# Splitting the first load over two queues and trimming warm-ups and tail of a gated attention and token-mixer kernel

## The chip, the cores and the metric

The kernel runs on one core of one Trainium2 chip. The metric is the device time of one execution in microseconds (us). The engines are named as in the profile: PE is TensorE's matmul side, PEld its weight loads, DVE is VectorE, ACT is ScalarE, POOL is GpSimd, and SP is SyncE, which here does nothing but issue transfers. An engine name with a q behind it (SPq, ACTq) is its sequencer, which issues transfers and waits.

## The reference

One input `x` of 2048 rows by 512 columns (bf16) goes through two blocks, and a gate mixes the results. Cut to what matters:

```python
x = A_x                                                # [1, 2048, 512]
g = sigmoid((x * gate_w).sum(-1, keepdims=True))
# block A: linear attention, 32 heads of 16
q, k, v = heads(x @ wqkv)
pq, pk = phi(q), phi(k)          # phi(t) = where(t > 0, t + 1, exp(t)) + 1e-6
kv, z = sum_s(pk * v), sum_s(pk)
a = ((pq @ kv) / (pq @ z + 1e-6)) @ wo
# block B: layer norm, then an MLP over the rows (tokens)
u = gelu(einsum("bsd,sf->bdf", layernorm(x), w1) + b1)   # f = 1792
b = transpose(einsum("bdf,fs->bds", u, w2) + b2)
out = g * a + (1 - g) * b
```

## The kernel before, in words

The 2048 rows are 16 tiles of 128 rows (`NT`), the 512 columns 4 chunks of 128 (`ND`). The order of all instructions is written out by hand, each engine runs its own in that order, and semaphores join them. There are four stages on PE:

1. For every row tile `t`: `k_part` multiplies the tile by Wk (four matmuls of 128x512, one for each chunk of Wk, into a bank `kacc`), `k_phi` turns it into `pk` on ACT and DVE, and `g_tile`, four tiles later, adds x^T pk into four banks `gacc`.
2. Three banks of the MLP's first layer (`uacc`) together with the q projection (`q_block`).
3. The rest of the first layer, and with it the small matmuls that fold Wv and Wo into `W2sb`.
4. For every row tile: four matmuls `aps` (attention) and 14 matmuls `yps` (the MLP's second layer), a DVE operation that mixes both into `ot` (line 501), and the store of `ot` (line 505). The last tile is done in column pieces, so that the last mix and store are short.

`k_part` needs the tile transposed (`xT`) as the stationary operand. Tiles 2 to 15 arrive transposed by transposing transfers that SP issues (`load_xT`, line 132). The first two tiles (`HEADS = 2`) are loaded plainly (`load_x`, line 126, into `xs`) and transposed on PE against the identity matrix (`transpose_part`, tile `pt`), then copied from PSUM to `xT` by DVE or ACT (`copy_part`, lines 203 and 205). The loop that does this:

```python
    for t in range(HEADS):
        for k0, k1 in ((0, 1), (1, 2), (2, ND)):
            transpose_part(t, k0, k1)
            copy_part(t, k0, k1, (t, k0) in ((0, 2), (1, 1)))
        k_part(0, range(2) if t == 0 else (2,))
    k_part(1, range(2))
    k_part(0, (3,))
```

So PE's order is: warm-up matmuls; transposes of tile 0; kacc of tile 0 with Wk's chunks 0 and 1; transposes of tile 1; kacc of tile 0 with chunk 2; kacc of tile 1 with chunks 0 and 1; kacc of tile 0 with chunk 3; kacc of tile 1 with chunks 2 and 3; tile 2. The warm-ups (`warm_up`, line 186) multiply a constant of ones into a bank that nobody reads. They need no transfer and run while the first ones are under way.

Transfers are issued from two queues, SP and ACT. SP issues x tile 0, x tile 1, Wk chunk 3, then the transposing loads; ACT issues Wk chunks 0 and 1 in one transfer, then chunk 2, then loads its table of functions (line 189). Below, x0 and x1 are the two plain x tiles, xT2 to xT5 the transposing loads that begin with tiles 2 to 5.

Of the kernel before, what the change touches and what calls it, by code (L numbers as in the profile page):

```python
# [15 lines left out]
def kernel(  # L16
# [13 lines left out]
    nc = tc.nc  # L30
    P = nc.NUM_PARTITIONS
# [6 lines left out]
    S, D = X.shape  # L38
    F = B_w1.shape[1]
    NT = S // P  # L40
# [12 lines left out]
    x_view = X.rearrange("(t p) d -> p t d", p=P)  # L53
# [12 lines left out]
    def keep(shape, dtype, name):  # L66
        return persist.tile(shape, dtype, name=name, tag=name)

    def bank(name, dtype=FP32):
        return ps.tile([P, SC], dtype, name=name, tag="bank")  # L70

    xs = keep([P, NT, D], BF16, "xs")
# [36 lines left out]
    def mm(o, lhsT, rhs, start, stop, **kw):  # L109
        nc.tensor.matmul(o, lhsT=lhsT, rhs=rhs, start=start, stop=stop, **kw)  # L110
# [14 lines left out]
    def load_x(q, t0, n):  # L125
        q.dma_start(out=xs[:, t0 : t0 + n, :], in_=x_view[:, t0 : t0 + n, :])

    def load_wk(q, k, n):
        q.dma_start(out=wk_sb[:, k : k + n, :], in_=wqkv_view[:, k : k + n, D : 2 * D])
# [3 lines left out]
            out=xT[:, :, t0 * P : (t0 + n) * P], in_=X[t0 * P : (t0 + n) * P, :], transpose=True  # L133
        )

    load_x(nc.sync, 0, 1)
    load_wk(nc.scalar, 0, 2)
    load_x(nc.sync, 1, 1)
    load_wk(nc.scalar, 2, 1)
    load_wk(nc.sync, 3, 1)  # L140
    for t in (2, 3, 4):
        load_xT(t, 1)
    nc.vector.memset(ones_f[:], 1.0)
# [3 lines left out]
        out=ident[:], in_=ident[:], compare_op=ALU.not_equal, fill=1.0, base=0,  # L147
# [5 lines left out]
        out=maskQ[:], in_=maskH[:].rearrange("p (a m) -> p m a", m=2), op=ALU.max, axis=AX.X  # L153
# [30 lines left out]
    def warm_up(n, cols=SC):  # L184
        for _ in range(n):
            mm(wps[:, :cols], warm[:, 0:P], warm[:, :cols], True, True)

    act_warm = keep([P, 1], FP32, "act_warm")
    nc.scalar.activation(out=act_warm[:], in_=ones_f[:], func=ACT.Exp)
    warm_up(6)  # L190

    pts = {}

    def transpose_part(t, k0, k1):
        pt = pts[t, k0, k1] = bank("pt")
        for k in range(k0, k1):
            mm(pt[:, k * P : (k + 1) * P], xs[:, t, k * P : (k + 1) * P], ident[:], True, True)

    def copy_part(t, k0, k1, on_act):
        src = pts.pop((t, k0, k1))[:, k0 * P : k1 * P].rearrange("p (k s) -> p k s", k=k1 - k0)  # L200
        dst = xT[:, k0:k1, t * P : (t + 1) * P]
        if on_act:
            nc.scalar.activation(out=dst, in_=src, func=ACT.Copy)
        else:
            nc.vector.tensor_copy(out=dst, in_=src)  # L205
# [13 lines left out]
    def k_part(t, ks):  # L219
        if t not in kaccs:  # L220
            kaccs[t] = bank("kacc")
        for k in ks:
            mm(
                kaccs[t][:], xT[:, k, t * P : (t + 1) * P], wk_sb[:, k, :],
                k == 0, k == ND - 1,
            )
# [55 lines left out]
    for t in range(HEADS):  # L282
        for k0, k1 in ((0, 1), (1, 2), (2, ND)):
            transpose_part(t, k0, k1)
            copy_part(t, k0, k1, (t, k0) in ((0, 2), (1, 1)))
        k_part(0, range(2) if t == 0 else (2,))
    k_part(1, range(2))
    k_part(0, (3,))
# [94 lines left out]
    def den_block(c, j):  # L383
        seg = pqT[:, j, c * SC : (c + 1) * SC]
        pz = work.tile([P, SC], FP32, name="pz", tag="pz", bufs=2)
        nc.scalar.activation(out=pz[:], in_=seg, func=ACT.Copy, scale=zcol[:, j : j + 1])  # L386
        nc.vector.transpose(out=zT[:], in_=pz[:])  # L387
        den = work.tile([P, SC // HEAD], FP32, name="den", tag="den", bufs=1)
        nc.vector.tensor_reduce(  # L389
            out=den[:], in_=zT[:].rearrange("p (a d) -> p a d", d=HEAD), op=ALU.add, axis=AX.X  # L390
        )
        rd = work.tile([P, SC // HEAD], BF16, name="rd", tag="rd", bufs=1)
        with nc.allow_low_precision(reason="the normalizer is used in bf16"):
            nc.vector.reciprocal(out=rd[:], in_=den[:])
        rex = work.tile([P, SC], BF16, name="rex", tag="rex", bufs=1)
        nc.vector.transpose(  # L396
            out=rex[:].rearrange("p (a d) -> p a d", d=HEAD),
            in_=rd[:].unsqueeze(2).to_broadcast([P, SC // HEAD, HEAD]),
        )
        nc.vector.tensor_tensor(out=seg, in0=seg, in1=rex[:], op=ALU.mult)  # L400
# [42 lines left out]
    for j in range(NB0, NF):  # L443
# [3 lines left out]
        for t in range(NT):  # L447
            if i == 2 and t < BRIDGE:
                for q in range(0, P, Q32):
                    c0 = jj * P + q  # L450
# [24 lines left out]
        out=gg[:], in0=gth[:], scalar1=0.5, scalar2=0.5, op0=ALU.mult, op1=ALU.add  # L475
    )
    nc.vector.tensor_scalar(
        out=c1[:], in0=gth[:], scalar1=-0.5, scalar2=0.5, op0=ALU.mult, op1=ALU.add
# [3 lines left out]
    for t in range(NT):  # L482
        c, tl = divmod(t, TPC)
        aps = bank("aps")
        for j in range(ND):
            mm(aps[:], pqT[:, j, t * P : (t + 1) * P], W2sb[:, j, :], j == 0, j == ND - 1)
        a_sc = work.tile([P, D], FP32, name="a_sc", tag="a_sc", bufs=2)
        nc.scalar.activation(  # L488
            out=a_sc[:], in_=aps[:], func=ACT.Identity,
            scale=gg[:, t : t + 1], bias=c2[:, t : t + 1],  # L490
        )
        for c0, W in ((0, 2 * P), (2 * P, P), (3 * P, P)) if t == NT - 1 else ((0, D),):
            cs = slice(c0, c0 + W)
            yps = bank("yps")
            for f in range(NF):
                mm(
                    yps[:, :W], w2c[c][:, f, tl * P : (tl + 1) * P], uT[:, f, cs],
                    f == 0, f == NF - 1,
                )
            ot = opool.tile([P, D], BF16, name="ot", tag="ot")  # L500
            nc.vector.scalar_tensor_tensor(  # L501
                out=ot[:, :W], in0=yps[:, :W], scalar=c1[:, t : t + 1], in1=a_sc[:, cs],
                op0=ALU.mult, op1=ALU.add,
            )
            (nc.scalar if t < 2 else nc.sync).dma_start(out=o_view[:, t, cs], in_=ot[:, :W])
        if t < NSC * ND - NDB:
            den_block(*divmod(t + NDB, ND))
# [30 lines left out]
```

## Time and profile before

| | us |
|---|---|
| median of 3 runs (162.43 to 162.89) | 162.76 |
| the profiled execution, its own time | 162.26 |
| its span, first to last instruction | 160.6 |
| PE matmuls busy | 155.9 (97% of the span) |
| DVE busy | 124.3 (77%) |
| ACT busy | 72.7 (45%) |
| PE warm-ups, six | 0.85 to 3.57 |
| start of the first transpose on PE | 3.36 |
| start of tile 2's kacc matmuls | 6.20 |
| start of the last DVE mix | 157.82 |

Times inside the execution count from the span's start. A matmul's bar in the trace is longer than the distance to the next one, because matmuls are pipelined: 128x512 matmuls have bars of 379 ns and start 216 ns apart. Of a transfer the profile gives the start of its issue and the time from there to its landing.

### The profile page before, as it was taken

What the parts mean: (1) busy time and instruction counts of PE and PEld (TensorE: products, weight loads), DVE (VectorE), ACT (ScalarE), POOL (GpSimd) and SP (SyncE); (2) the same over time, 40 slices, a digit from 0 to 9 for tenths busy, and PEclk for the clock granted to TensorE, in tenths of its full rate; (3) what the DMA queues carried; (4) which work ended last, traced back from release to release, by engine and by line L of the source; (5) the groups of instructions that cost most, each with busy time, mean ns of one, the idle gap of its engine ahead of it and who ended that gap; (6) DMA issues with size and microseconds to landing.
All of it is one profiled execution on the core that took longest, in us unless ns stands there. A gap on an engine that the chain in (4) does not pass through costs nothing.

```text
span 160.6 us, 2228 instructions
## 1 busy us (share of the span) xinstructions
PE 155.9 (97%) x822; PEld 72.5 (45%) x836; DVE 124.3 (77%) x274; ACT 72.7 (45%) x113; POOL 7.3 (5%) x17
## 2 busy tenths in 40 slices
PE   7999999999999999999999999999999999999993
PEld 2444444444444445444444444444444444444462
DVE  1599999769999998756999999676999999711122
ACT  3543486654978393059873320237333442111110
POOL 3000332002010000000000000000000000000000
PEclk9999999999999999999999999999999999999999
DMA  5699999999970007600930679401000001110001
GB/s 168 150 231 262 328 352 329 354 349 348 336 171 0 0 0 257 204 0 4 356 101 2 213 244 306 151 33 37 33 33 33 33 33 58 48 61 33 33 33 33
DMA packets 29929, 23.07 MB, mean 144 GB/s; under 512 B 8384, under 2 KB 29888, under 8 KB 29920
## 3 DMA queue, kind: packets, MB, share of 16 engines
q1 hardware_dynamic: 29104, 22.15, 45.2%
q10 hardware_dynamic: 704, 0.66, 1.2%
q0 software_dynamic: 112, 0.14, 0.4%
q8 instruction: 6, 0.10, 0.3%
q14 instruction: 3, 0.02, 0.0%
HBM read 19.01 MB, written 2.10 MB: 131 GB/s over the span
## 4 chain that ended last, share of the span: by engine, by line
PE 84%; DVE 13%; issue 1%; ACT 0%
PE yps L110 30%; PE uacc L110 24%; PE kacc L110 9%; PE gacc L110 9%; PE aps L110 9%; DVE pqT L213 6%; DVE zacc L274 3%; DVE stats L233 2%; DVE e L210 2%; PE wps L110 2%; PE qacc L110 1%; DVE mv L234 1%; ACT e L209 0%; PE kvps L110 0%; PE w2ps L110 0%
## 5 line engine op out<-in xcount | busy, mean ns | idle before, releaser
L110 PE MATMUL uacc<-hs,w1c 128*128 128x512 bf16 (+1 forms) x227 | 50.8, 379 | 0.4 <-issue 0.2
L110 PE MATMUL yps<-uT,w2c 128*128 128x512 bf16 (+2 forms) x247 | 50.8, 355 | 0.3
L110 PEld LDWEIGHTS <-w2c 128*128 128x128 bf16 x252 | 23.6, 98 | 25.2
L110 PEld LDWEIGHTS <-w1c 128*128 128x128 bf16 (+1 forms) x233 | 21.8, 98 | 26.0 <-issue 0.2
L488 ACT ACTIVATE a_sc<-aps,c,gg 128x512 f32<-128x512 f32 x16 | 12.4, 775 | 31.2 <-PE aps L110 15.5
L501 DVE SCALAR_TENSOR_TENSOR ot<-yps,c,a_sc 128x512 bf16<-128x512 f32 (+2 forms) x18 | 12.3, 688 | 15.3 <-PE yps L110 11.7
L322 ACT ACTIVATE uT<-uacc,bcol 128x512 bf16<-128x512 f32 x14 | 9.3, 686 | 17.5 <-PE uacc L110 17.4
L110 PE MATMUL qacc<-xT,wq_sb 128*128 128x512 bf16 x64 | 16.4, 379 | 0.1
L110 PE MATMUL aps<-W2sb,pqT 128*128 128x512 bf16 x63 | 16.4, 379 | 0.1
L110 PE MATMUL kacc<-wk_sb,xT 128*128 128x512 bf16 x63 | 15.9, 379 | 0.2 <-DVE xT L205 0.2
L387 DVE STREAM_TRANSPOSE zT<-pz 128x512 f32<-128x512 f32 x16 | 11.3, 705 | 6.0 <-ACT pz L386 6.0
L110 PE MATMUL gacc<-pk,xs 128*128 128x512 bf16 x63 | 15.7, 379 | 0.1
L249 ACT ACTIVATE hs<-xs,nmr,rstd 128x512 bf16<-128x512 bf16 x16 | 12.8, 805 | 2.3 <-DVE nmr L243 2.3
L209 ACT ACTIVATE e<-kacc 128x512 bf16<-128x512 f32 x16 | 9.4, 594 | 9.7 <-PE kacc L110 8.5
L386 ACT ACTIVATE pz<-pqT,zcol 128x512 f32<-128x512 bf16 x16 | 11.4, 715 | 4.8 <-DVE ot L501 4.7
L209 ACT ACTIVATE e<-qacc 128x512 bf16<-128x512 f32 x16 | 9.5, 594 | 7.7 <-PE qacc L110 7.7
L396 DVE STREAM_TRANSPOSE rex<-rd 128x512 bf16<-128x512 bf16 x16 | 11.4, 711 | 0.6
L213 DVE SCALAR_TENSOR_TENSOR pqT<-qacc,e 128x512 bf16<-128x512 f32 x16 | 11.1, 692 | 0.6
L213 DVE SCALAR_TENSOR_TENSOR pk<-kacc,e 128x512 bf16<-128x512 f32 x16 | 11.1, 692 | 0.6
L389 DVE TENSOR_REDUCE den<-zT 128x32 f32<-128x512 f32 x16 | 11.0, 686 | 0.6
L210 DVE TENSOR_SCALAR e<-e 128x512 bf16<-128x512 bf16 x32 | 9.0, 282 | 2.5 <-ACT e L209 2.5
L233 DVE BATCH_NORM_STATS2 stats<-xs 128x6 f32<-128x512 bf16 x16 | 10.9, 683 | 0.0
(58 smaller groups left out, 96.2 us busy)
## 6 DMA issues: line engine op xcount, KB each, us to landing
w2c<-in_B_w_dram SPq DMA_DIRECT2D x8, 896.0 KB, 5.7
w1c<-in_B_w_dram SPq DMA_DIRECT2D x3, 2048.0 KB, 14.0
out_dram<-ot SPq DMA_DIRECT2D x13, 128.0 KB, 1.7
xs<-in_A_x_dram SPq DMA_DIRECT2D x1, 1024.0 KB, 6.6
w1c<-in_B_w_dram SPq DMA_DIRECT2D x1, 1024.0 KB, 15.3
xs<-in_A_x_dram SPq DMA_DIRECT2D x1, 512.0 KB, 5.0
wq_sb<-in_A_wqkv_dram SPq DMA_DIRECT2D x1, 512.0 KB, 5.6
wv_sb<-in_A_wqkv_dram SPq DMA_DIRECT2D x1, 512.0 KB, 12.3
```

The source lines that it names most:

```text
L110: nc.tensor.matmul(o, lhsT=lhsT, rhs=rhs, start=start, stop=stop, **kw)
L209: nc.scalar.activation(out=e[:], in_=acc[:], func=ACT.Exp)
L210: nc.vector.tensor_scalar(out=e[:], in0=e[:], scalar1=1.0, scalar2=PHI_EPS, op0=ALU.min, op1=ALU.add)
L213: nc.vector.scalar_tensor_tensor(out=dst, in0=acc[:], scalar=0.0, in1=e[:], op0=ALU.max, op1=ALU.add)
L233: nc.vector.bn_stats(out=stats[:], in_=xs[:, t, :])
L249: nc.scalar.activation(out=hs[:, t, :], in_=xs[:, t, :], func=ACT.Identity, scale=rstd[:, t : t + 1], bias=nmr[:, t : t + 1],)
L386: nc.scalar.activation(out=pz[:], in_=seg, func=ACT.Copy, scale=zcol[:, j : j + 1])
L387: nc.vector.transpose(out=zT[:], in_=pz[:])
L389: nc.vector.tensor_reduce(out=den[:], in_=zT[:].rearrange("p (a d) -> p a d", d=HEAD), op=ALU.add, axis=AX.X)
L396: nc.vector.transpose(out=rex[:].rearrange("p (a d) -> p a d", d=HEAD), in_=rd[:].unsqueeze(2).to_broadcast([P, SC // HEAD, HEAD]),)
L488: nc.scalar.activation(out=a_sc[:], in_=aps[:], func=ACT.Identity, scale=gg[:, t : t + 1], bias=c2[:, t : t + 1],)
L501: nc.vector.scalar_tensor_tensor(out=ot[:, :W], in0=yps[:, :W], scalar=c1[:, t : t + 1], in1=a_sc[:, cs], op0=ALU.mult, op1=ALU.add,)
```

## The change

There are four edits. The first x tile is loaded as two halves of 64 rows, one from SP and one from ACT. Behind it each queue issues one of Wk's first two chunks, SP then x tile 1, ACT then Wk's chunks 2 and 3 in one transfer. The warm-ups ahead of the transposes are four of 512 columns and one of 384 instead of six of 512, and one more of 256 columns stands between the first tile's transposes and its kacc matmuls. The last output tile is done in pieces of 384 and 128 columns instead of 256, 128 and 128.

```diff
-    load_x(nc.sync, 0, 1)
-    load_wk(nc.scalar, 0, 2)
+    for q, p0 in ((nc.sync, 0), (nc.scalar, P // 2)):
+        q.dma_start(out=xs[p0 : p0 + P // 2, 0, :], in_=x_view[p0 : p0 + P // 2, 0, :])
+    load_wk(nc.sync, 0, 1)
+    load_wk(nc.scalar, 1, 1)
     load_x(nc.sync, 1, 1)
-    load_wk(nc.scalar, 2, 1)
-    load_wk(nc.sync, 3, 1)
+    load_wk(nc.scalar, 2, 2)
     for t in (2, 3, 4):
         load_xT(t, 1)
@@
-    warm_up(6)
+    warm_up(4)
+    warm_up(1, 384)
@@
             copy_part(t, k0, k1, (t, k0) in ((0, 2), (1, 1)))
+        if t == 0:
+            warm_up(1, 256)
         k_part(0, range(2) if t == 0 else (2,))
@@
-        for c0, W in ((0, 2 * P), (2 * P, P), (3 * P, P)) if t == NT - 1 else ((0, D),):
+        for c0, W in ((0, 3 * P), (3 * P, P)) if t == NT - 1 else ((0, D),):
```

## The prediction

> **What bounds the kernel now.** I read the page first: the share of each engine, then who TensorE (PE) waits for, then the first 7 us and the last 7 us of the timeline, then each early transfer's time to landing.
>
> ```profile
> PE 155.9 (97%) x822; PEld 72.5 (45%) x836; DVE 124.3 (77%) x274; ACT 72.7 (45%) x113; POOL 7.3 (5%) x17
> ```
>
> ```profile
> PE wps L110 <- PEq L522: 0.8, 1, 0.8
> PE kacc L110 <- DVE xT L205: 0.2, 1, 0.2
> PE uacc L110 <- issue: 0.2, 1, 0.2
> ```
>
> PE is busy 97% of the span, and its waits (last three rows) come to 1.2 us, of which 0.8 is the start of the program. So PE's queue is one unbroken chain: what moves the point from which it never waits again moves the end by the same amount. That point lies in the first microseconds of the timeline (columns: start, duration, engine and what it runs; in brackets the idle time before and what ended it):
>
> ```profile
> 0.85 2.72 PE L110 MATMUL wps<-const-bfloat16-1.0 128*128 128x512 bf16 x6 [0.85 <-PEq L522]
> 3.19 0.53 PEld L110 LDWEIGHTS <-xs 128*128 128x128 bf16 x4 [0.53 <-DMA xs<-in_A_x_dram]
> 3.36 0.53 PE L110 MATMUL pt<-ident,xs 128*128 128x128 bf16 x4
> 4.06 0.60 PE L110 MATMUL kacc<-wk_sb,xT 128*128 128x512 bf16 x2 [0.17 <-DVE xT L205]
> 4.50 0.39 PE L110 MATMUL pt<-ident,xs 128*128 128x128 bf16 x4
> 4.72 4.22 PE L110 MATMUL kacc<-wk_sb,xT 128*128 128x512 bf16 x18
> ```
>
> Six warm-ups hold PE to 3.36, although the x tile was there at 3.15 (the weight load of row 2 starts at 3.19). Then come four transposes, two kacc matmuls, the second tile's transposes at 4.50, kacc of Wk's chunk 2 at 4.72, and one more copy wait to 5.11; tile 2's first kacc matmul starts at 6.20 and nothing interrupts after it. Measure of the clock: warm-ups start 427 ns apart, kacc matmuls 216 ns; by the spacing of the four transposes the change comes at 3.65, 2.80 us after the first matmul.
>
> What feeds that stretch, as issue and time to landing (four windows of the DMA view):
>
> ```profile
> wk_sb<-in_A_wqkv_dram ACTq DMA_DIRECT2D x1, 256.0 KB, 3.1
> xs<-in_A_x_dram SPq DMA_DIRECT2D x1, 128.0 KB, 2.3
> ...
> xs<-in_A_x_dram SPq DMA_DIRECT2D x1, 128.0 KB, 3.0
> wk_sb<-in_A_wqkv_dram ACTq DMA_DIRECT2D x1, 128.0 KB, 3.3
> ...
> wk_sb<-in_A_wqkv_dram SPq DMA_DIRECT2D x1, 128.0 KB, 3.3
> ```
>
> With issues at 0.81, 0.81, 1.27, 1.30 and 1.73 the landings in the trace are: x0 3.15, Wk 0-1 3.87, x1 4.28, Wk 2 4.61, Wk 3 5.04. The same sums for the transposing loads, which SP issues 1.3 us apart from 2.20: xT2 5.75, xT3 6.31, xT4 7.54, xT5 9.27. Wk 2 is used 0.11 us after it lands, Wk 3 (at 5.55) 0.5 us after. The windows show what limits the landings:
>
> ```profile
> 1.80:2.20 0.40, 0.40 (x3) 0.13 (x2) 0.13 (x1) 0.38 (x1) 0.38 (x2) 1.00 0.49 125
> 2.20:2.60 0.40, 0.40 (x3) 0.12 (x2) 0.03 (x1) 0.40 (x1) 0.00 (x0) 1.00 0.78 246
> 2.60:3.00 0.40, 0.40 (x3) 0.06 (x1) 0.00 (x0) 0.40 (x1) 0.00 (x0) 1.00 1.03 356
> 3.40:3.80 0.40, 0.40 (x5) 0.32 (x3) 0.09 (x1) 0.00 (x0) 0.00 (x0) 1.00 1.09 382
> ...
> 89.70:90.10 0.40, 0.40 (x4) 0.20 (x2) 0.40 (x1) 0.28 (x1) 0.00 (x0) 1.00 0.62 184
> ```
>
> The last two columns are the DMA engines' share and GB/s. From 2.6 on the engines are full (356 to 382 GB/s) and only the bytes ahead of a transfer count; before that is a ramp at half rate. The last row, a W2 load that starts on idle engines from one queue, ramps in the same way.
>
> **The warm-ups.** 3072 columns become 2432: 640 columns at 427 ns per 512 is 0.53 us, so PE is free at 2.83 instead of 3.36. Behind them PE waits for both halves of x0. The other warm-up, 256 columns behind the first transposes, is 0.21 us at the slow rate; the first kacc waits 0.70 us after the first transpose (3.36 to 4.06) for the copy, the transposes take 0.43 of it, and it fits in the 0.27 left: nothing, as long as those 0.70 stay. The most that this part can give is 0.53.
>
> **x0 in two halves.** The bytes of x0 stay at 128 KB, and it now goes ahead of all of Wk. Call r the time by which the early transfers land sooner. Bounds: r = 0 if 16 engines work off the same rows in the same ramp; r = 0.6 if there were no ramp (x0's rows run from 1.84 to 2.79 in the trace; at 356 GB/s 128 KB need 0.37). I take 0.2, near the lower end, since the ramp shows in the single-queue load at 89.7 too, so it is not peculiar to x0, while Wk's 256 KB no longer compete in the first half microsecond. It could also be below nothing: one more transfer to complete, and PE waits for the later of two.
>
> The Trainium skill, "DMA: Bandwidth & Descriptors", section "Rules for kernel authors", speaks against this part: two transfers to disjoint partition halves serialize on the same 16 engines, one 128-partition transfer is better. By it r would be 0 and the sum below would end 0.2 later; no run so far shows two halves.
>
> **Wk and the order of queues.** SP's issues: x0a, Wk 0, x1, then xT2; ACT's: x0b, Wk 1, Wk 2-3. SP still makes three issues of 0.46 us before xT2, so the transposing loads keep their times to about 0.05. ACT makes three instead of two: its table load (1.28 us) starts at 2.3 instead of 1.82, so its first copy (0.38) can run from 3.85 and end at 4.25. That copy feeds the chunk-2 matmul; the landing of Wk 2 (below) covers it, and without that cover it would hold PE at 4.3. The 384 KB ahead of x1 are the same as before (x0 and Wk 0-1), so x1 lands at 4.28 - r. But Wk 2 and 3 are now one 256 KB transfer with one completion: chunk 2, which PE wants right behind the second transposes, comes with chunk 3, after the same 768 KB that stood before 5.04. It lands at 5.04 - r instead of 4.61.
>
> **Walking PE through it, r = 0.2.** x0 at 2.95, first transpose 3.0, first kacc 3.70, Wk 1 (3.87 - 0.2) is there, second kacc 3.93; x1 at 4.08, so the second transposes run at 4.14, with PE ready for Wk 2 at 4.37. Wk 2-3 land at 4.84, PE resumes at 4.88. The second tile's copies (0.61 us behind its transposes, 4.50 to 5.11) are done by 4.75. Six kacc matmuls of 216 ns remain to tile 2: 6.17, against 6.20. The 0.53 us of warm-ups turn into a wait for Wk: gain 0.03. With r = 0 it is 6.37, a loss of 0.18; with r = 0.4 5.97, a gain of 0.22.
>
> **The tail.** The last tile's 14 matmuls of 256 columns take 1.53 us and each 14 of 128 take 0.78 (starts 154.53, 156.06, 156.84). 384 columns lie between 109 and 216 ns a matmul: 162 ns, 2.27 us in place of 2.31. Gain 0.04. DVE's piece of 384 (0.62, between 0.48 and 0.75) ends at about 157.67, and the last piece starts at 157.79; SP's output issue (0.33) ends 0.1 before the last one. If either ran over, it would cost up to 0.1.
>
> **Sum.** -0.03 - 0.04 = -0.07 us. The profiled execution took 162.26 (span 160.6 and 1.66 around it), which becomes 162.19; the median is 162.76, 0.5 above, so the forecast is 162.7. That is no change: a difference of 0.3%, 0.49 us, is about what a measurement of this kernel can tell from none.
>
> **Rivals.** *Faster.* Two queues halve the ramp, r is 0.45 or more: PE then goes as early as the transposing loads allow. xT4 lands at 7.54, its matmul starts at 7.92; xT5 at 9.27 for 9.65. The gain stops at 0.34, up to 0.4 if SP's shorter first issue moves them; with the tail 162.3 to 162.4. For it: the ramp is real. Against: the row at 89.7.
>
> *Slower, x1 behind Wk 2-3.* ACT's third issue and SP's third start within 0.1 us of each other (about 1.70 on SP, 1.80 on ACT, by intervals of 0.46 and 0.49 to 0.52). If ACT's goes first, x1 lands where Wk 3 did, 5.04; transposes 5.08, copies to 5.69, where 5.11 was: 0.58 late, less the tail, 163.3. It decides when x1 lands later than 4.8. Against: landings so far follow the order of issue.
>
> *Slower, the clock.* Before the rate changes at 3.65, PE has run without a gap for 2.80 us. Now it idles between 2.83 and the landing of x0, 0.1 to 0.4 us. If a gap starts the count anew at 3.0, the fast rate comes at 5.8: the first four kacc matmuls and the second transposes run at half rate, to 5.85, four matmuls follow, and tile 2 starts at 6.71, 0.5 late: 163.2. It decides if such a gap counts at all; the 0.39 us between transposes and kacc, after the change, undid nothing. The Trainium skill, "TensorE: Matmul & The Clock Gate", Part 1, has a free-running window of about 3.4 us of activity that releases the clock; a full busy window cannot be needed, since the change came here after 2.80 us. Were a whole window lost, an estimate from that page's figure is twelve matmuls at the slow rate, 1.2 late, 163.9, which lies outside my range.
>
> **Chances.** Main case 0.55 (162.45 to 163.0), faster case 0.2, x1 late 0.13, clock 0.12. The faster case straddles the bound at 162.27; half of it and 0.1 from the scatter of the main case make 0.2 faster. Most of both slow cases, which end near the bound at 163.25 or beyond, and 0.05 from the main case's late end make 0.3 slower; 0.5 stay within 0.3%. The range runs from 162.2, the faster case, to 163.5, which takes in the late x1 and the shorter clock case.
>
> **What would show it.** Right: transposes at about 3.0, a wait of 0.3 to 0.7 us of kacc for Wk ahead of the third kacc matmul, tile 2 at 6.0 to 6.4, last output matmul about 0.04 nearer to the start of its tile. Wrong: Wk 2-3 landing before 4.5 with PE held by an xT load instead (faster), x1 landing after 4.8, or kacc matmuls 427 ns apart beyond 4 us (slower).

## The result, and the profile after

The changed kernel is slower: 165.15 us in the median of 6 runs (163.85 to 165.94), where before stands at 162.51 in the same comparison. The ratio is 1.0147, 95% interval 1.0113 to 1.0182, so about 2.4 us (the medians of these few runs lie 2.6 apart). The forecast of 162.7 and its range up to 163.5 missed. Ratios, here and below, are of fast runs: of one kernel, the halves by columns, two runs of ten stand over 1.5% above its fastest and are left out of its ratio. The profiled execution took 165.94 (span 164.2), 3.6 us more span than the one of before.

First the waits of PE (who waited for whom: total, times, longest), after:

```profile
PE wps L110 <- PEq L526: 0.8, 1, 0.8
PE pt L110 <- DMA xs<-in_A_x_dram: 0.8, 2, 0.5
PE kacc L110 <- DMA wk_sb<-in_A_wqkv_dram: 0.4, 1, 0.4
PE uacc L110 <- issue: 0.2, 1, 0.2
```

Where PE had one short wait for a copy, it now waits three times for transfers. (The view counts a wait from the modelled end of the matmul before it; by starts the gaps are larger.) The timeline shows the two queues and PE:

```profile
0.81 0.58 SPq L137 DMA_DIRECT2D xs<-in_A_x_dram  x1
0.81 0.57 ACTq L137 DMA_DIRECT2D xs<-in_A_x_dram  x1
...
1.41 1.08 ACTq L129 DMA_DIRECT2D wk_sb<-in_A_wqkv_dram  x2
1.45 0.83 SPq L129 DMA_DIRECT2D wk_sb<-in_A_wqkv_dram  x1
...
2.33 0.41 SPq L126 DMA_DIRECT2D xs<-in_A_x_dram  x1
...
3.49 0.59 PE L110 MATMUL pt<-ident,xs 128*128 128x128 bf16 x4 [0.46 <-DMA xs<-in_A_x_dram]
...
4.66 1.01 PE L110 MATMUL kacc<-wk_sb,xT 128*128 128x512 bf16 x2 [0.37 <-DMA wk_sb<-in_A_wqkv_dram]
...
6.03 0.61 PE L110 MATMUL pt<-ident,xs 128*128 128x128 bf16 x4 [0.36 <-DMA xs<-in_A_x_dram]
```

Three things differ from what the prediction took for granted. The two issues of half an x tile take 0.58 and 0.57 us, longer than a whole tile's 0.40, and the ordinary issue behind one takes up to 0.83, where 0.41 to 0.49 stood. So x1 is issued at 2.33, where I had 1.70, and ACT's Wk 2-3 (2.03) goes ahead of it. And the first transposes start at 3.49, later than before, in spite of shorter warm-ups.

The windows (last two columns: share of the DMA engines, GB/s) show that much less is then moved, where before 356 GB/s and more were reached from 2.6 on:

```profile
2.60:3.00 0.40, 0.40 (x2) 0.00 (x0) 0.00 (x0) 0.40 (x1) 0.00 (x0) 1.00 0.75 192
3.40:3.80 0.40, 0.31 (x4) 0.34 (x5) 0.01 (x1) 0.40 (x1) 0.00 (x0) 1.00 0.93 159
```

In these two stretches they move 192 and 159 GB/s, against 356 and 382 (between them 320, against 382). The engines still count as busy, 0.75 and 0.93, because single packets take long. In the DMA view of 3.4 to 3.8, 74 packets of ACT's queue take 51.5% of the time of 16 engines before, 45 ns each; after, six packets take 40.7%, 430 ns each on average. What held them the trace does not say.

The landings in the trace: x0's halves 3.05 and 3.35 (3.15 before), Wk 1 3.77, Wk 0 4.61, x1 5.98 (4.28), Wk 2-3 5.99 (Wk 2: 4.61, Wk 3: 5.04). The chain that ended last, from 0 to 12 us, names the transfer:

```profile
2.33 3.65 DMA xs<-in_A_x_dram
5.98 0.05 issue
6.03 0.61 PE pt L110 x4
6.63 5.53 PE kacc L110 x16
```

The last row holds the second half of the loss. In the groups of the page kacc matmuls have a mean bar of 426 ns (second row) where they had 379 (first row, before):

```profile
L110 PE MATMUL kacc<-wk_sb,xT 128*128 128x512 bf16 x63 | 15.9, 379 | 0.2 <-DVE xT L205 0.2
L110 PE MATMUL kacc<-wk_sb,xT 128*128 128x512 bf16 x63 | 18.3, 426 | 0.4 <-DMA wk_sb<-in_A_wqkv_dram 0.4
```

By their starts they stand 427 ns apart until 10.70 and 216 after: the fast rate comes 7 us later than the 3.65 of before. (The columns PEclk do not show this; they read full speed throughout.) The sum for the profiled execution: the second transposes start 1.53 us later (6.03 for 4.50); ten kacc matmuls and four transposes behind them run at the slow rate, 10 x 0.211 + 0.2 = 2.3, and the copy wait of before, 0.17, is hidden. That is 3.65, which is what the first gacc matmul shows (12.43 for 8.79) and what is handed on to the end of the span (3.64).

### The profile page after: what moved, and what is told of

Read it like the earlier page. It is cut to its first block, busy times and chain, and to the rows that moved or that the text cites. A ratio compares the mean times of both kernels' runs of the same rounds, so it can differ in the third digit from the quotient of the medians.

```text
span 164.2 us, 2199 instructions
## 1 busy us (share of the span) xinstructions
PE 158.5 (97%) x808; PEld 72.3 (44%) x822; DVE 124.2 (76%) x273; ACT 72.8 (44%) x113; POOL 7.3 (4%) x17
## 4 chain that ended last, share of the span: by engine, by line
PE 81%; DVE 13%; DMA 2%; issue 1%; SPq 1%; ACT 0%
PE yps L110 29%; PE uacc L110 23%; PE kacc L110 9%; PE gacc L110 8%; PE aps L110 8%; DVE pqT L215 5%; DVE zacc L276 3%; DMA xs<-in_A_x_dram 2%; DVE stats L235 2%; DVE e L212 2%; PE qacc L110 1%; DVE mv L236 1%; SPq L129 1%; PE pt L110 0%; ACT e L211 0%
## 5 line engine op out<-in xcount | busy, mean ns | idle before, releaser
L110 PEld LDWEIGHTS <-w2c 128*128 128x128 bf16 x238 | 22.8, 98 | 25.9
L110 PE MATMUL kacc<-wk_sb,xT 128*128 128x512 bf16 x63 | 18.3, 426 | 0.4 <-DMA wk_sb<-in_A_wqkv_dram 0.4
L110 PEld LDWEIGHTS <-xs 128*128 128x128 bf16 x72 | 7.0, 101 | 10.0 <-DMA xs<-in_A_x_dram 2.5
```

## The experiments

Every time is compared with runs of before on the same chip. Two theories stood at the start. *C*: the loss is mainly the late fast rate, brought on by PE's idle time. *T*: the late transfers alone make it.

**Loads alone.** The new loads, with the warm-ups and the tail of before.

```diff
-    load_x(nc.sync, 0, 1)
-    load_wk(nc.scalar, 0, 2)
+    for q, p0 in ((nc.sync, 0), (nc.scalar, P // 2)):
+        q.dma_start(out=xs[p0 : p0 + P // 2, 0, :], in_=x_view[p0 : p0 + P // 2, 0, :])
+    load_wk(nc.sync, 0, 1)
+    load_wk(nc.scalar, 1, 1)
     load_x(nc.sync, 1, 1)
-    load_wk(nc.scalar, 2, 1)
-    load_wk(nc.sync, 3, 1)
+    load_wk(nc.scalar, 2, 2)
```

> The new order of loads alone, with the six warm-ups and the tail of before. Theory C (most of the loss is the clock: PE's gap between the shorter warm-ups and x0 postpones the fast rate): warm-ups run to 3.36, the rate changes near 3.65 as before, and only the later landings cost; from the trace of after x1 lands at about 6.0 instead of 4.3, so about +1.5 us, 164.0. Theory T (the late transfers alone make the loss, the slow rate only follows from them): the same as the whole change, 165.2. If the issues from two queues did not disturb each other after all: 162.5.

Measured: 164.17 (163.78 to 165.71), ratio 1.0112 (1.0057 to 1.0166). The loads by themselves carry most of the loss, as far as four runs tell. In this profile the transposes start at 3.36 as before, but Wk holds PE at 5.17 and 6.71, and the fast rate is there from 4.9 on.

**Warm-ups alone.**

```diff
-    warm_up(6)
+    warm_up(4)
+    warm_up(1, 384)
...
+        if t == 0:
+            warm_up(1, 256)
```

> The shorter warm-ups alone (four of 512, one of 384, one of 256 behind the first transposes), with the loads and tail of before. Theory C: PE idles from 2.83 to 3.19, the rate changes one window of some 3.5 us later or more, kacc at 427 ns until about 7, +1.2 to +2 us: 163.7 to 164.5. Theory T: x0 lands at 3.15, PE starts up to 0.17 earlier, 162.4 to 162.6.

Measured: 162.77, ratio 1.0003 (0.9984 to 1.0021). C's number is wrong here: PE idles for about 0.3 us before x0 and nothing is lost. Nothing is won either; in the profile the first kacc starts at 4.02, when Wk 0-1 is there (3.98), and what follows runs at the slow rate to 5.39. A rival of mine, that this gap alone would cost 0.5 us or more, falls.

**The whole change with PE kept busy.**

```diff
-    warm_up(4)
-    warm_up(1, 384)
+    warm_up(7)
...
+        if t == 1:
+            warm_up(3)
...
-            warm_up(1, 256)
+            warm_up(1, 512)
```

> The whole change, but with PE kept busy: seven warm-ups of 512 ahead of the first transposes, one of 512 behind them and three of 512 ahead of the second tile's transposes. Theory C: the rate changes near 3.65, the transfers still cost about 1.5: 164.0, and kacc matmuls stand 216 ns apart from the first one. Theory T: no better than the whole change, 165.2 or later.

Measured: 164.41 (164.03 to 165.02), ratio 1.0122 (1.0086 to 1.0157). No run reaches the 165.5 to 165.9 of half of the runs of the whole change, which is C's side; four runs are few for that. The fast rate came at 5.24, not at 3.65. About 2 us stay. Most of that is the transfers: x1 lands at 5.85, and the added warm-ups themselves hold the second transposes from there to 6.10.

**The split alone.** x0's halves, then Wk and x1 on the queues of before.

```diff
-    load_x(nc.sync, 0, 1)
+    for q, p0 in ((nc.sync, 0), (nc.scalar, P // 2)):
+        q.dma_start(out=xs[p0 : p0 + P // 2, 0, :], in_=x_view[p0 : p0 + P // 2, 0, :])
```

> The split of x0 alone: two halves from SP and ACT, then Wk 0-1, x1, Wk 2, Wk 3 on the queues of before, warm-ups and tail of before. If it is the two simultaneous issues that cost (0.58 us each in the trace of after where 0.40 and 0.46 stood), x1 is issued 0.2 to 0.5 later and lands at 4.6 to 5.0, and tile 2 starts 0.3 to 0.6 later: 162.9 to 163.2. If it is the order of Wk instead, no change: 162.5.

Measured: 165.49 (164.47 to 166.09), ratio 1.0169 (1.0119 to 1.0219), far more than expected. The two lines of the split cost as much as the whole change. The issues again take 0.58 and 0.57, ACT's next one 0.85, and Wk 0-1 lands at 5.95 instead of 3.87, so that PE stands from 3.78 to 5.99. The fast rate is there when it goes on (second row below):

```profile
3.36 0.63 PE L110 MATMUL pt<-ident,xs 128*128 128x128 bf16 x4
5.99 0.59 PE L110 MATMUL kacc<-wk_sb,xT 128*128 128x512 bf16 x2 [2.00 <-DMA wk_sb<-in_A_wqkv_dram]
```

In this kernel x1, issued at 1.44 behind SP's half, lands at 3.81, earlier than before (4.28): it is not always the same transfer that comes late. What is slow about it: 64 rows (*R*), or two queues that begin with a half (*Q*)?

**Halves by columns.** Against the split alone:

```diff
-    for q, p0 in ((nc.sync, 0), (nc.scalar, P // 2)):
-        q.dma_start(out=xs[p0 : p0 + P // 2, 0, :], in_=x_view[p0 : p0 + P // 2, 0, :])
+    for q, c0 in ((nc.sync, 0), (nc.scalar, D // 2)):
+        q.dma_start(out=xs[:, 0, c0 : c0 + D // 2], in_=x_view[:, 0, c0 : c0 + D // 2])
```

> x0 in two halves from SP and ACT as in split_only, but cut by columns: each half has all 128 rows, 256 columns of each. Theory R (a transfer to 64 partitions is slow to issue): the first issues take 0.40 to 0.46 us again, x1 is issued near 1.27 and lands near 4.4; ACT's Wk comes one issue later, so 162.5 to 163.2. Theory Q (two queues that begin with a half each, and one more transfer, are slow whatever the cut): issues of 0.58 and 0.85 as in split_only, 164.5 or more.

Measured: 163.4, ratio 1.0073 (1.0028 to 1.0118), in two groups: six runs from 162.97 to 163.47, four from 165.18 to 165.69 (the ratio is without the highest two). The lower group lies at the upper end of what R was given, the upper one above Q's bound. The queues, by columns:

```profile
0.80 0.41 ACTq L137 DMA_DIRECT2D xs<-in_A_x_dram  x1
0.81 0.40 SPq L137 DMA_DIRECT2D xs<-in_A_x_dram  x1
1.24 0.99 ACTq L129 DMA_DIRECT2D wk_sb<-in_A_wqkv_dram  x2
1.27 0.41 SPq L126 DMA_DIRECT2D xs<-in_A_x_dram  x1
```

**Both 64-row halves on one queue.** Against the split alone:

```diff
-    for q, p0 in ((nc.sync, 0), (nc.scalar, P // 2)):
-        q.dma_start(out=xs[p0 : p0 + P // 2, 0, :], in_=x_view[p0 : p0 + P // 2, 0, :])
+    for p0 in (0, P // 2):
+        nc.sync.dma_start(out=xs[p0 : p0 + P // 2, 0, :], in_=x_view[p0 : p0 + P // 2, 0, :])
```

> x0 as two halves of 64 rows, both from SP; ACT begins with Wk 0-1 as before, SP goes on with x1 and Wk 3. Theory R: SP's two first issues take 0.58 each, x1 is issued at 2.0 or later and lands above 5: 163.5 to 164.5. Theory Q: SP's issues take 0.40 to 0.46, x1 is issued at 1.74 and lands near 4.4: 162.6 to 163.0.

Measured: 165.68 (165.18 to 166.01), ratio 1.0193 (1.016 to 1.0227). The queues:

```profile
0.80 1.00 ACTq L129 DMA_DIRECT2D wk_sb<-in_A_wqkv_dram  x2
0.81 1.21 SPq L137 DMA_DIRECT2D xs<-in_A_x_dram  x2
2.06 0.58 SPq L126 DMA_DIRECT2D xs<-in_A_x_dram  x1
```

With the same bytes, halves by columns are issued in 0.40 and 0.41 on two queues at once; halves by 64 rows take 0.58 and 0.57 on a queue of their own, and so does the x1 behind them (0.58), while ACT's issues beside them keep their usual 0.5. For the issues this is R. The time itself is 1.2 us above what R was given; with x0 late, the fast rate comes only at 9.7 in this profile. x0 lands at 4.30 and 4.97 here, and at 2.9 and 3.06 by columns. On two queues the 64-row halves landed 2.2 and 2.5 us after the start of their issues (whole change; 2.3 for the whole tile before), here 3.5, behind Wk 0-1, which was issued in 0.48 beside them and landed at 4.00, ahead of x0.

**Wk 2 and 3 merged, alone.**

```diff
-    load_wk(nc.scalar, 2, 1)
-    load_wk(nc.sync, 3, 1)
+    load_wk(nc.scalar, 2, 2)
```

> Loads of before with one difference: Wk's chunks 2 and 3 in one transfer from ACT. By the step of the prediction, they land together near 5.0, chunk 2 is wanted at 4.72, tile 2 starts 0.1 to 0.3 later; the transposing loads are issued 0.46 earlier, which brings nothing: 162.6 to 163.0. If the merge were a main part of the loss: above 163.5.

Measured: 162.9, ratio 1.0016 (0.9997 to 1.0035): as the prediction had it, with Wk 2-3 landing at 4.99 and the third kacc at 5.03, where 4.72 stood.

**The whole change without the split.**

```diff
-    for q, p0 in ((nc.sync, 0), (nc.scalar, P // 2)):
-        q.dma_start(out=xs[p0 : p0 + P // 2, 0, :], in_=x_view[p0 : p0 + P // 2, 0, :])
-    load_wk(nc.sync, 0, 1)
-    load_wk(nc.scalar, 1, 1)
-    load_x(nc.sync, 1, 1)
-    load_wk(nc.scalar, 2, 2)
+    load_x(nc.sync, 0, 1)
+    load_wk(nc.scalar, 0, 1)
+    load_wk(nc.sync, 1, 1)
+    load_wk(nc.scalar, 2, 2)
+    load_x(nc.sync, 1, 1)
```

> The whole change without the split: x0 in one transfer from SP, Wk 0 from ACT, Wk 1 and x1 from SP, Wk 2-3 from ACT, the shorter warm-ups and the tail of 384 and 128. Theory S (the split is the cause of the loss): issues of 0.4 to 0.5, 162.5 to 163.1. If Wk's new order or the shorter warm-ups carry the loss: 163.8 or more, as the whole change.

Measured: 163.68 (163.25 to 165.05), ratio 1.0071 (1.003 to 1.0112), between the two expectations. ACT, with one issue less ahead, now issues Wk 2-3 at 1.25 and SP x1 at 1.73; x1 lands at 5.30 behind it and the second transposes start at 5.35, 0.85 late. This is the prediction's rival of x1 behind Wk 2-3, in a kernel of its own.

**The gap filled.** Halves by columns as above, and PE busy while it waits for Wk:

```diff
             copy_part(t, k0, k1, (t, k0) in ((0, 2), (1, 1)))
+        if t == 0:
+            warm_up(2)
```

> column_halves with two more warm-ups of 512 columns behind the first tile's transposes, where PE waited 0.75 us for Wk. The runs of column_halves fall into two groups, 163.0 to 163.5 (six) and 165.2 to 165.7 (four). Theory C (the upper group is a fast rate that comes a window or two late, because PE was idle in the window): with the gap filled no run is above 164.5, median 163.0 to 163.5. If the upper group comes from the transfers: it stays, in about four runs of ten.

Measured: 163.55 (163.05 to 163.99), ratio 1.0035 (1.0018 to 1.0052). None of 12 runs is in the upper group, where four of ten were; chance alone would do that about 3 times in 100. The transfers land within 0.2 us of those of the column cut, so the upper group goes with PE's idle time of 0.76 us ahead of the first kacc. That it is the clock's is likely but was not seen, since no run of the upper group was profiled. The lowest run, 163.05, is still 0.8 above the lowest of before (162.29), with the gap filled: that is mainly the transfers' part.

**Two warm-ups.** Before with four warm-ups less.

```diff
-    warm_up(6)
+    warm_up(2)
```

> Before with two warm-ups instead of six, transfers untouched: PE idles from 1.70 to x0's landing at about 3.1. Theory C: the fast rate comes late in many runs, 164 to 165.5, kacc matmuls 427 ns apart to 6 us or beyond. If gaps don't count and only time since the first matmul does: 162.5 to 163.0.

Measured: 163.95 (163.19 to 164.74), ratio 1.0067 (1.0045 to 1.009). PE idles from about 1.7 to 3.21; kacc matmuls stand 427 ns apart to 7.4. Idle time with untouched transfers costs 1.1 us, just under the lower end of C and without its 165s.

**The whole change with halves by columns.** The one difference from the whole change is the cut.

```diff
-        q.dma_start(out=xs[p0 : p0 + P // 2, 0, :], in_=x_view[p0 : p0 + P // 2, 0, :])
+        q.dma_start(out=xs[:, 0, c0 : c0 + D // 2], in_=x_view[:, 0, c0 : c0 + D // 2])
```

> The whole change with one difference: the halves of x0 are cut by columns (128 rows, 256 columns each) instead of by 64 rows. Theory R (64-row transfers are slow to issue, and what follows them): first issues of 0.40, x1 issued at 1.7 instead of 2.3, landing near 5.0 instead of 6.0; lower group at 162.8 to 163.4, with some runs 2 us above it from the clock. Without R: as the whole change, lower group 163.9.

Measured: 163.34, ratio 1.0037 (1.0012 to 1.0063); nine of ten runs from 162.97 to 163.67, one at 165.31. The cut by 64 rows thus makes 1.1% of the 1.47%, about 1.8 us. (That is a difference of two ratios from two comparisons, good to some 0.4%.) x1 is issued at 1.72 and lands at 4.89. In the profile of this kernel the first kacc still waits for Wk, to 4.32, and the second transposes start at 5.12: transfers that land later than before make the remaining 0.6 us, together with the clock (fast rate from 5.6).

**The tail alone.**

```diff
-        for c0, W in ((0, 2 * P), (2 * P, P), (3 * P, P)) if t == NT - 1 else ((0, D),):
+        for c0, W in ((0, 3 * P), (3 * P, P)) if t == NT - 1 else ((0, D),):
```

> The tail of 384 and 128 columns alone. By the step of the prediction 0.04 us sooner, which a comparison of medians can't tell from nothing; the time from the last tile's first yps matmul to the end of the span should be 0.03 to 0.05 shorter: 6.03 instead of 6.07.

Measured: 163.07, ratio 1.0001 (0.9982 to 1.0019). From the last tile's last aps matmul to its last yps matmul 3.216 us pass, 3.252 before: 0.04 sooner, as forecast, and too little for the medians to tell. By the measure that was named, from the first yps matmul to the end of the span, nothing is gained: 6.07, against 6.03 before. The last store is issued 0.04 sooner but lands at the same distance from that matmul (5.11 before, 5.10 here). The profile of this run has a use beyond its question (PE's timeline):

```profile
3.36 0.63 PE L110 MATMUL pt<-ident,xs 128*128 128x128 bf16 x4
4.05 1.03 PE L110 MATMUL kacc<-wk_sb,xT 128*128 128x512 bf16 x2
4.88 0.63 PE L110 MATMUL pt<-ident,xs 128*128 128x128 bf16 x4
5.31 1.91 PE L110 MATMUL kacc<-wk_sb,xT 128*128 128x512 bf16 x5
```

The start is that of before, to the instruction and to 0.01 us up to 4.05. But here the matmuls stay 427 ns apart until 6.6, and the execution took 163.53 where the profiled one of before, with the fast rate from 3.65, took 162.26. The moment of the fast rate is not a property of the kernel.

No kernel here beats the one of before.

## Why the prediction was wrong, point by point

**What held.** That PE's first 6 us set the end: every shift of the first gacc matmul is found again at the end of the span (3.65 in, 3.64 out; in all fourteen profiles to within 0.3). The tail: 0.04 forecast, 0.04 measured on PE, of which nothing was left at the end, and DVE's piece of 384 took 0.62 as estimated. The merge of Wk 2 and 3: 5.04 - r forecast, 4.99 measured. That shorter warm-ups only turn into a wait for Wk: no change when done alone.

**The step that failed first** is "SP still makes three issues of 0.46 us before xT2". An issue was priced by the rows of 128-row transfers, and the 64-row one was even given a gain ("SP's shorter first issue"). It takes 0.58, and the issue behind it 0.56 to 0.86. x1 was issued at 2.33 instead of 1.70, and xT2 at 2.79 instead of 2.20.

**The step that failed with it** is "only the bytes ahead of a transfer count". From it x1 was put at 4.28 - r, that is 4.08, and it landed at 5.98: issued 0.63 late, and then 3.65 us on the way where 2.38 were allowed. Wk 2-3 going ahead explains 0.76 of that by the prediction's own rows (5.04 for 4.28). The rest it does not explain: the same 768 KB were through at 5.99, not at 5.04 - r.

**The term r** stands for that step. It had bounds of 0 and 0.6 and I took 0.2, with one clause that it could also be below nothing and no price for that. It was below: the last of the early transfers landed at 5.99 instead of 5.04, r = -0.95. Halves by columns still give -0.4 (Wk 2 at 5.47 as the last of the same bytes). The missing bound would have been the cost of a stretch at a low rate, and the rows for it stood in the prediction's own window view: the ramp at 125 and 246 GB/s. In the whole change low rates last until 4.2 us (187 GB/s from 3.8 to 4.2). The slow issues have a large part in that; what of it comes from the larger number of smaller transfers, as in the column cut with its normal issues, was not separated.

The Trainium skill, "DMA: Bandwidth & Descriptors", "Rules for kernel authors", which spoke against the split, was right in its advice. Its reason, that the halves serialize on the same engines, would give r = 0; the measured loss is larger, and begins with the issue of 64-row transfers.

**The rival of x1 behind Wk 2-3** came true in the whole change, but by a cause not thought of: not because ACT's third issue was early (2.03, 0.23 later than I had it), but because SP's was 0.63 late. Its price of 0.58 was too small; x1 landed at 5.98, not 5.04. The order is not all of it either: with the loads alone SP's x1 went first (2.06, ACT's third at 2.30) and still landed at 5.46.

**The rival of the clock** came true as well, and not as told. The fast rate is not counted from PE's first matmul: with the same start it came at 3.65 in one execution and at 6.6 in another. A gap of 0.3 us before x0 does nothing (ratio 1.0003). But idle time while the rate is still slow makes it possible to miss the change again, until 9.7 (both halves on one queue) or 10.7 (the whole change). In the main sum the clock stood at nothing. The rival's price, 0.5, was counted from a restart at 3.0; the profile shows 2.1 on the kacc matmuls alone, and the two groups of the column cut stand 2.3 apart. What the Trainium skill's "TensorE: Matmul & The Clock Gate", Part 1, says of a window that runs freely and so differs from run to run agrees with 3.65 and 6.6 for one start, though the spread measured here is larger than the 0.5 us to either side that the part gives. I had used the page's window for a price beyond my range and let the trace's 2.80 us decide, which is one draw from a spread. That price does not come out either: twelve matmuls at 0.211 are 2.5 us, not 1.2, and nothing is said of what would hide the rest.

**The chances.** The two slow rivals were treated as alternatives of 0.13 and 0.12. They share a cause: a late x1 leaves PE idle, and idle PE keeps the slow rate. Added up they are 1.5 + 2.1, which no case held.

**What stays open.** Why a 64-row transfer is slow to issue, and slows the one behind it, was not found out. That the upper runs of the whole change (165.46 to 165.94) are the clock's rests on the profile of one of them (165.94, fast rate from 10.70); the filled version of the whole change had four runs only. How much idle time in which stretch delays the fast rate is settled only in part (last section): 0.3 us before x0 cost nothing, 0.76 behind it brought four runs of ten to 165, 1.5 before it cost 1.1 on average.

## What to carry to other kernels

Price an issue by a row of the same shape, and where there is none, leave room for it to be slower. A transfer cut by rows is not half a transfer; if a first tile must be cut for two queues, cut its columns and keep all 128 partitions. Here even that was slower than no cut, by 0.73% alone and 0.35% with the gap filled. In a kernel whose start is a race between loads and warm-ups, let PE do idle work until the loads have arrived: a wait there can cost more in clock than its own length.

## What the runs showed of the hardware

Among the first loads, issues of 64-row transfers of 64 KB from SP or ACT took 0.57 to 0.58 us, of 128-row transfers of 64 or 128 KB 0.40 to 0.43 from SP; the 128-row issue behind a 64-row one on its queue took 0.56 to 0.86. The first loads of the kernel before moved 125 GB/s from 1.8 to 2.2, 246 from 2.2 to 2.6 and 356 from then on; a later load on idle DMA engines moved 184 in the 0.4 us from 89.7 and 302 in the next.

The fast rate of PE came at 3.65 and at 6.6 with the same instructions and loads, worth 1.1 us at the first gacc matmul (8.79 and 9.86). The kernel of before ranged from 162.29 to 163.41 in 35 runs, a spread of the same size; it would fit that the profiled execution, with its early change, lay 0.5 below the median shown.

The traces say more of when that change comes. Twelve of the fourteen hold a record of the granted clock, which begins at the change (3.65 before, 10.70 in the whole change); the fast stretch in it lasts 157.013 us in ten kernels and 153.600 in two, that is 46 and 45 times 3.4133. Count back from the change in steps of 3.413 us, and take a matmul of 512 columns at the slow rate as 0.427 us of work:

| | change at | busy in the step before it | in earlier steps |
|---|---|---|---|
| before | 3.65 | 82% | |
| tail alone | 6.64 | 92% | 70% |
| merge alone | 3.47 | 77% | |
| whole change by columns | 5.63 | 74% | 40% |
| both halves on one queue | 9.69 | 100% | 41%, 59% |
| whole change | 10.70 | 100% | 67%, 69% |

In all twelve the step that ended in the change was 74 to 100% busy, and no earlier step more than 70%. This fits a clock that is judged at fixed steps of 3.413 us, which fall differently on every execution: in the tail alone a step ended at 3.22, too early for its 70%, where before's ended at 3.65. It was read from traces that were there, and no run was made to test it; counted by the longer bars instead, the two ranges overlap (77% and up, 79% and down). It does not explain the upper group of the column cut, where a step with just the gap of 0.76 us in it would still be 78% busy.
